# Score visits of one key chunk between second products, and two first-product tiles begun early at the seam of batch 0

## The chip, the cores and the metric

The kernel runs on one core of a Trainium2 chip. The metric is the device time of one execution in microseconds, the median of several runs. TensorE is called PE, its weight loads PEld, VectorE DVE, ScalarE ACT, GpSimd POOL. A program on one core has no second die to compare with. All runs used here were classed as fast; the few in which the granted clock was visibly below 1 are named where they matter.

## The reference

Attention with one added to the softmax denominator, followed by a two-layer network with a squared ReLU:

```python
scores = scale * np.matmul(q, k.transpose(0, 1, 3, 2))        # 8 batches, 12 heads, 448 x 64
m = np.max(scores, axis=-1, keepdims=True)
e = np.exp(scores - m)
attn = e / (np.sum(e, axis=-1, keepdims=True) + np.exp(-m) + 1e-09)
x = np.matmul(attn, v) ...                                    # as 3584 tokens x 768
h = x @ w_in                                                  # 768 x 2048, "first products"
r = np.maximum(h, 0.0)
return (r * r) @ w_out                                        # 2048 x 768, "second products"
```

## The kernel before

Heads are worked in pairs, six per batch, and the keys of a pair in four chunks of 112. A "visit" computes scores of some chunks into PSUM tiles named `sp` (two buffers); an exp on ACT empties each. First products are tiles of twelve matmul steps (six where a tile spans all 448 queries) into `mp` (three buffers), emptied by a ReLU (`rt`) and a square (`gs`) on DVE. Where one tile ends and the next begins is called a tile boundary below: there a product needs a free `mp` buffer.

Two parts matter. First, twelve stages, each of three pairs, in which visits alternate with second products. One step of a second product is two matmuls on the upper and lower 64 rows of the array ("row halves"); the scores use row halves too. Everything before and after a stage (values, first products, row sums) runs in "column halves", 64 columns of the array at a time.

```python
    for i in range(3 * NPAIR, NU, 3):
        b, pr = units[i][0:2]
        for j in range(3):
            begin(i + j)
            scores(units[i + j], ets[i + j], 0)          # chunks 0 and 1
            if j:
                add(i + j - 1, 1, 2)
            rows(10 if j < 2 else 9)                     # steps of second products
            scores(units[i + j], ets[i + j], 1)          # chunks 2 and 3
            add(i + j, 0)
            if j < 2:
                rows(10 if j < 1 else 9)
        mode[0] = COLS2
        for at in pending:
            take_in(at)                                  # values, normalised
        ...
```

Second, the seam: batch 0 is worked in two parts (queries 0 to 191, then 192 to 447), and when the first part is normalised its first products are queued and drained in portions between the attention groups that follow, up to the end of batch 1.

```python
        if i == NPAIR:                                   # the seam
            ...
            normalise(two, xp, rcp)
            scores(u, et, 1)
            keep_warm(2)                                 # two dummy matmuls
            queue(0, FIRST)
            share[0] = left() / (NPAIR + 4)
        else:
            for at in transpose_at.get(i, ()):
                transposes(*at)                          # each holds one mp buffer until DVE copies it
            if i == NPAIR + 1:
                scores(u, et, 1)
                values_of(i - 1, xp)
            drain(share[0] * 0.45)
            ...
```

At the end of batch 1 the queue must be empty before the first row-half stage begins (the second products need it):

```python
        for step in range(3):
            add_chunks(u, et, es, half, step)
            drain(share[0] * (0.15, 0.1, 0.15)[step])
        if i == 3 * NPAIR - 1:
            run(ins, len(ins))
            rcps[i] = row_sums([u], (ess.pop(i)[0:1],))
```

The softmax here doesn't subtract the row's maximum and nothing guards it: scores larger than these inputs give would overflow.

Of the kernel before, what the change touches and what calls it, by code (L numbers as in the profile page):

```python
# [9 lines left out]
FP16 = mybir.dt.float16  # L10
AF = mybir.ActivationFunctionType
ALU = mybir.AluOpType
# [3 lines left out]
def kernel(  # L16
# [9 lines left out]
    nc = tc.nc  # L26
# [114 lines left out]
            )  # L141


    def cast(b, pr, names="qk"):
        for name in names:
            f = flat.tile([P, 2, RUN, D], FP16, name=f"flat{name}")
            if pr < 2 and name == "k":
                nc.scalar.activation(out=f, in_=naturals[name, b, pr], func=AF.Copy)
            else:
                nc.vector.tensor_copy(f, naturals[name, b, pr])  # L150
            naturals[name, b, pr] = f

    def transposes(b, pr, between=None):
        tp = mp_tile(FP16)
        for i, name in enumerate("qk"):
            for s in range(RUN):
                for h in range(2):
                    nc.tensor.transpose(tp[64 * h:64 * h + 64, i, P * s:P * s + P],
                                        naturals[name, b, pr][:, h, s, :], ident[0:P, 0:P])
        if b not in qks:  # L160
            qks[b] = qk_pool.tile([128, 3, COLS], FP16, name="qk")
        if between:
            between()
        parts = (0, S // 2, S) if b == 0 and pr < 2 else (0, S)
        for x, y in zip(parts, parts[1:]):
            nc.vector.tensor_copy(qks[b][:, 0:2, pr * S + x:pr * S + y], tp[:, :, x:y])  # L166

# [9 lines left out]
            return et[:, 0:RUN * 2 * n].rearrange("p (c h j n) -> p c h j n", c=2, h=2, j=2)[:, c, :, kk % 2, :]  # L177
        return et.rearrange("p (k x) -> p k x", k=RUN)[:, kk]

    def scores(u, et, c):  # L180
        b, pr, q0, n = u
        qk = qks[b]
        two = [] if n == S else s_psum.tile([P, 2, 512], FP32, name="sp")
        for kk in (2 * c, 2 * c + 1):
            sp = s_psum.tile([P, 2, 512], FP32, name="sp") if n == S else two
            if b in ON_PE:
                o = 0 if n == S else kk % 2 * n
                for h in range(2):
                    r = slice(64 * h, 64 * h + 64)
                    x = pr * S  # L190
                    nc.tensor.matmul(sp[:, h, o:o + n], qk[r, 1, x + P * kk:x + P * kk + P],  # L191
                                     qk[r, 0, x + q0:x + q0 + n], start=True, stop=True)
            else:
                for h in range(2):
                    for odd in range(2):
                        r = slice(64 * odd, 64 * odd + 64)
                        x = (2 * pr + h) * (S // 2)
                        kx = x + kk // 2
                        which = 1
                        if kk % 2 != odd:  # L200
                            which = 2
                            kx += kk % 2
                        nc.tensor.matmul(sp[:, odd, h * (S // 2):(h + 1) * (S // 2)],  # L203
                                         qk[r, which, kx:kx + 2 * P - 1:2], qk[r, 0, x:x + S // 2],
                                         start=True, stop=True)
            if n == S:
                exp(chunk(et, u, c, kk).rearrange("p (o x) -> p o x", o=2), sp[:, :, 0:S])
        if n < S:
            exp(et[:, 0:RUN * 2 * n].rearrange("p (c h x) -> p c h x", c=2, h=2)[:, c], two[:, :, 0:2 * n])
# [74 lines left out]
    def product(out_, lhsT, rhs, start, stop):  # L284
# [4 lines left out]
        else:  # L289
            nc.tensor.matmul(out_, lhsT, rhs, start=start, stop=stop)  # L290

    def tile_in(t0, n, f0, per):

        xt, x0 = xts[t0 // S], t0 % S
        m = per * n
        hp = mp_tile()
        for j in range(per):
            fb = f0 + j
            for dc in range(DCH):
                product(hp[:, j * n:(j + 1) * n], win[:, dc, fb * 128:(fb + 1) * 128],  # L300
                        xt[:, dc, x0:x0 + n], start=(dc == 0), stop=(dc == DCH - 1))
                if j < per - 1 or dc < DCH - 1:
                    yield n / 2.4
        rt = r_pool.tile([128, 512], FP16, name="rt")
        nc.vector.tensor_scalar(out=rt[:, 0:m], in0=hp[:, 0:m], scalar1=0.0, scalar2=None, op0=ALU.max)  # L305
        r = rt[:, 0:m].rearrange("p (j n) -> p j n", j=per)
        nc.vector.tensor_mul(gs[:, f0:f0 + per, t0 % RING:t0 % RING + n], r, r)  # L307
        yield n / 2.4

    def store(c, ot, n0, n1):  # L310
        end = c + 128
# [68 lines left out]
    def queue(t0, n):  # L380

        per = max(1, 512 // n)
        for f0 in range(0, NFFB, per):
            ns = per * DCH * n / 2.4
            ins.append([ns, ns, tile_in(t0, n, f0, per)])

# [20 lines left out]
    def drain(ns):  # L407
        while ins and ns > 0:
            ns -= one(ins)
# [16 lines left out]
    def keep_warm(n):  # L426
        wp = m_psum.tile([128, 512], FP32, name="mp")
        for _ in range(n):
            nc.tensor.matmul(wp, warm[:, 0:128], warm, start=True, stop=True)
# [27 lines left out]
    def sums_of(at):  # L457
        return row_sums(units[at:at + 2], (ess.pop(at)[0:1], ess.pop(at + 1)[0:1]))

    def values_of(at, xp):  # L460
        values(units[at], ets.pop(at), xp, at % 2 * units[at][3])
# [9 lines left out]
    for i in range(NPAIR):  # L471
        u, et, es, half = begin(i)
        mode[0] = COLS2
        scores(u, et, 0)
        if i < 2:
            scores(u, et, 1)
        if i in (3, 5):
            rcp = sums_of(i - 3)
        if i == 0:
            transposes(0, 1, lambda: cast(0, 2, "q"))  # L480
            cast(0, 2, "k")
        else:
            for at in transpose_at.get(i, ()):
                transposes(*at)
        if i == 0:
            keep_warm(1)
        if i:
            sums(i - 1)
        if i > 1:
            scores(u, et, 1)  # L490
        if i in (2, 4):
            xp = x_psum.tile([128, 512], FP32, name="xp")
        if i in (2, 3, 4):
            values_of(i - 2, xp)
        if i == 4:
            values_of(3, xp)
        if i in (3, 5):
            normalise(units[i - 3:i - 1], xp, rcp)
        if i in (1, 3, 5):
            keep_warm(1 + i // 5)  # L500


    for i in range(NPAIR, 2 * NPAIR):
        u, et, es, half = begin(i)
        two = units[i - 2:i] if i % 2 == 0 else None
        if i % 2 or i == NPAIR:
            xp = x_psum.tile([128, 512], FP32, name="xp")
        mode[0] = COLS2
        scores(u, et, 0)
        if i == NPAIR:  # L510
            sums(i - 1)
            values_of(i - 2, xp)
            values_of(i - 1, xp)
            rcp = sums_of(i - 2)
            normalise(two, xp, rcp)
            scores(u, et, 1)
            keep_warm(2)
            queue(0, FIRST)
            share[0] = left() / (NPAIR + 4)
        else:  # L520
            for at in transpose_at.get(i, ()):
                transposes(*at)
            if i == NPAIR + 1:
                scores(u, et, 1)
                values_of(i - 1, xp)
            drain(share[0] * 0.45)
            if i > NPAIR + 1:
                scores(u, et, 1)
                values_of(i - 1, xp)
            if two:  # L530
                rcp = sums_of(i - 2)
            drain(share[0] * 0.3)
        add_chunks(u, et, es, half, 1)
        if two and i > NPAIR:
            normalise(two, xp, rcp)
        add_chunks(u, et, es, half, 2)
        if i > NPAIR:
            drain(share[0] * 0.25)
        if i == NPAIR + 5:
            load_natural(2, 0, 3)  # L540
            for n0 in (0, HALF):
                for j in range(2):
                    load_wout(n0, j, 2)
# [44 lines left out]
    def rows(n):  # L588
        mode[0] = ROWS2
        while outs and n > 0:  # L590
            one(outs)
            n -= 1
        mode[0] = COLS2
# [6 lines left out]
    def add(at, *steps):  # L600
        for step in steps:
            add_chunks(units[at], ets[at], *ess[at], step)
# [5 lines left out]
    for i in range(3 * NPAIR, NU, 3):  # L608
        b, pr = units[i][0:2]
        for j in range(3):  # L610
            begin(i + j)
            scores(units[i + j], ets[i + j], 0)
            if j:
                add(i + j - 1, 1, 2)
            rows(10 if j < 2 else 9)
            scores(units[i + j], ets[i + j], 1)
            add(i + j, 0)
            if j < 2:
                rows(10 if j < 1 else 9)
        mode[0] = COLS2  # L620
        for at in pending:
            take_in(at)
# [61 lines left out]
```

## Time and profile before

| | before |
|---|---|
| median time, first 3 runs (range) | 416.72 us (416.47 to 416.76) |
| span in the profile | 415.0 us |
| PE busy | 404.1 us, 97% |
| a row-half stage (the 2nd to 12th) | 10.45 us, eleven times (10.42 the first of them) |
| the first row-half stage | 68.89 to 80.12 us |

PE works almost throughout, so the question is what its turns contain. A matmul's record is longer than its turn: the reader takes the start of one group in the timeline and the start of the next, and compares like with like. The prediction below shows those lines. A line of a timeline gives the start, the length, the engine, the line of kernel.py, what is written and read, and how many instructions are merged in it (x4); square brackets give the idle time before it and what ended it.

### The profile page before, as it was taken

The page shows a single profiled execution, that of the slowest core. Times are in us where ns is not written, and L with a number is a line of the kernel's source. Part 1 is how long each engine was busy: PE and PEld are TensorE (multiplying, and loading weights), DVE is VectorE, ACT ScalarE, POOL GpSimd, SP SyncE. Part 2 cuts the span into 40 slices and gives each one's busy share as a digit, 9 for nine tenths or more (in the row PEclk, how much of TensorE's full clock was granted, in tenths as well). Part 3 has the DMA queues.
Part 4 walks back from the last instruction along what each step waited for, and adds up shares of the span by engine and source line. Part 5 has one row for each costly group of instructions (what it writes and reads, how often), then busy time and mean ns, then how long its engine had stood idle before and what let it go on. Part 6 is the DMA issues. An engine that isn't in the chain of part 4 may idle for free.

```text
span 415.0 us, 10686 instructions
## 1 busy us (share of the span) xinstructions
PE 404.1 (97%) x4717; PEld 271.7 (65%) x4717; DVE 289.8 (70%) x553; ACT 232.9 (56%) x312; POOL 36.7 (9%) x58
## 2 busy tenths in 40 slices
PE   7888999999999999999999999999999999999997
PEld 3566666867576766767676676767667675555664
DVE  4767988887866787776976788767876888287000
ACT  5888987758384655648464665837555573100111
POOL 7524030010000110002000040001000000000000
PEclk9999999999999999999999999999999999999999
DMA  9999999489204992398503984198101010000222
GB/s 201 197 197 198 203 202 218 87 155 207 71 16 93 171 190 51 87 191 145 134 2 88 190 145 97 55 187 142 42 2 39 39 40 2 38 39 0 77 76 77
DMA packets 75823, 45.58 MB, mean 110 GB/s; under 512 B 42560, under 2 KB 72000, under 8 KB 75456
## 3 DMA queue, kind: packets, MB, share of 16 engines
q0 software_dynamic: 28848, 22.16, 35.1%
q1 hardware_dynamic: 46208, 22.05, 23.5%
q8 instruction: 37, 0.61, 0.6%
q10 hardware_dynamic: 720, 0.69, 0.6%
q14 instruction: 10, 0.08, 0.1%
HBM read 45.69 MB, written 17.93 MB: 153 GB/s over the span
## 4 chain that ended last, share of the span: by engine, by line
PE 88%; ACT 4%; DVE 3%; DMA 3%; POOL 1%; issue 0%; POOLq 0%
PE mp L288 24%; PE mp L334 17%; PE mp L290 10%; PE xp L288 8%; PE sp L203 6%; PE mp L238 5%; PE xp L334 5%; PE xp L290 3%; PE xp L238 3%; ACT et L171 3%; DMA vn<-in_v_dram 3%; PE sp L191 2%; PE mp L252 2%; ACT rcp L255 1%; POOL nn L99 1%; DVE rt L305 1%
## 5 line engine op out<-in xcount | busy, mean ns | idle before, releaser
L171 ACT ACTIVATE et<-sp 112x896 f16<-112x896 f32 (+2 forms) x144 | 124.2, 913 | 49.8 <-PE sp L203 37.8
L288 PEld LDWEIGHTS <-win 128*64 128x64 f16 x1536 | 85.3, 110 | 45.0 <-issue 2.1
L288 PE MATMUL mp<-xt,win 128*64 128x448 f16 (+2 forms) x1200 | 107.1, 323 | 1.2 <-DVE qk L166 1.2
L334 PE MATMUL mp<-wout,gs 64*128 64x384 f16 x896 | 104.4, 322 | 0.2 <-DVE rt L305 0.2
L334 PEld LDWEIGHTS <-gs 64*128 64x128 f16 x1152 | 69.1, 94 | 19.6 <-issue 0.6
L305 DVE TENSOR_SCALAR rt<-mp 128x448 f16<-128x448 f32 (+2 forms) x96 | 59.7, 622 | 25.6 <-PE mp L288 13.1
L307 DVE TENSOR_TENSOR gs<-rt 128x448 f16<-128x448 f16 (+2 forms) x128 | 50.2, 392 | 4.4
L334 PE MATMUL xp<-wout,gs 64*128 64x384 f16 x256 | 48.0, 322 | 0.0
L255 ACT ACTIVATE rcp<-mp,one_b 128x448 f32<-128x448 f32 (+2 forms) x42 | 26.5, 630 | 37.7 <-PE mp L252 37.7
L171 ACT ACTIVATE nn<-sp 112x896 f16<-112x896 f32 x48 | 41.4, 914 | 6.0 <-PE sp L203 4.3
L343 ACT ACTIVATE ot<-mp 128x384 f32<-128x384 f32 (+1 forms) x16 | 7.6, 477 | 62.1 <-PE mp L290 48.2
L203 PE MATMUL sp<-qk 64*112 64x224 f16 x480 | 36.6, 260 | 0.0
L288 PE MATMUL xp<-xt,win 128*64 128x448 f16 x336 | 36.5, 352 | 0.0
L203 PEld LDWEIGHTS <-qk 64*112 64x112 f16 x480 | 29.6, 127 | 7.4 <-issue 3.6
L290 PEld LDWEIGHTS <-gs 128*128 128x128 f16 x256 | 24.4, 98 | 15.1 <-issue 0.4
L238 PEld LDWEIGHTS <-vn 112*64 112x64 f16 x432 | 22.4, 109 | 15.8 <-issue 3.8
L290 PE MATMUL mp<-wout,gs 128*128 128x384 f16 (+1 forms) x192 | 30.3, 317 | 0.0
L256 ACT ACTIVATE rcp<-rcp 128x448 f32<-128x448 f32 (+2 forms) x48 | 27.7, 577 | 1.5
L216 DVE TENSOR_TENSOR es<-et 112x896 f16<-112x896 f16 x30 | 18.7, 622 | 13.9 <-ACT et L171 13.8
L191 PE MATMUL sp<-qk 64*112 64x448 f16 (+2 forms) x192 | 24.6, 321 | 2.4 <-ACT et L171 1.4
L218 DVE TENSOR_TENSOR es<-es,half 112x896 f16<-112x896 f16 x42 | 26.2, 623 | 0.9
L341 DVE TENSOR_SCALAR ot<-mp 128x384 f32<-128x384 f32 x28 | 15.6, 558 | 14.4 <-PE mp L334 10.9
(63 smaller groups left out, 346.0 us busy)
## 6 DMA issues: line engine op xcount, KB each, us to landing
vn<-in_v_dram POOLq DMA_DIRECT2D x7, 672.0 KB, 8.7
out_dram<-ot SPq DMA_DIRECT2D x9, 384.0 KB, 2.3
win<-in_moe_w_in_dram POOLq DMA_DIRECT2D x8, 384.0 KB, 14.1
wout<-in_moe_w_out_dram POOLq DMA_DIRECT2D x4, 768.0 KB, 17.6
stage_q<-in_q_dram POOLq DMA_DIRECT2D x4, 676.0 KB, 10.7
stage_k<-in_k_dram POOLq DMA_DIRECT2D x4, 676.0 KB, 13.6
out_dram<-ot SPq DMA_DIRECT2D x8, 288.0 KB, 8.8
out_dram<-ot SPq DMA_DIRECT2D x9, 192.0 KB, 2.6
```

The lines of the kernel that those rows point to most:

```text
L171: nc.scalar.activation(out=out_, in_=in_, func=AF.Exp, scale=scale)
L191: nc.tensor.matmul(sp[:, h, o:o + n], qk[r, 1, x + P * kk:x + P * kk + P], qk[r, 0, x + q0:x + q0 + n], start=True, stop=True)
L203: nc.tensor.matmul(sp[:, odd, h * (S // 2):(h + 1) * (S // 2)], qk[r, which, kx:kx + 2 * P - 1:2], qk[r, 0, x:x + S // 2], start=True, sto ...
L218: nc.vector.tensor_add(es, es, half[:, 0:2 * S])
L238: nc.tensor.matmul(xp[64 * h:64 * h + 64, o:o + n], vns[b][:, 2 * pr + h, kk, :], of_head(chunk(et, u, kk // 2, kk), u, h), start=(kk == 0 ...
L255: nc.scalar.activation(out=rcp[:, 0:m], in_=zp[:, 0:m], func=AF.Ln, bias=one_b)
L256: nc.scalar.activation(out=rcp[:, 0:m], in_=rcp[:, 0:m], func=AF.Exp, scale=-1.0)
L288: nc.tensor.matmul(out_[x:x + 64], lhsT[:, x:x + 64], rhs, start=start, stop=stop)
L290: nc.tensor.matmul(out_, lhsT, rhs, start=start, stop=stop)
L305: nc.vector.tensor_scalar(out=rt[:, 0:m], in0=hp[:, 0:m], scalar1=0.0, scalar2=None, op0=ALU.max)
L307: nc.vector.tensor_mul(gs[:, f0:f0 + per, t0 % RING:t0 % RING + n], r, r)
L334: nc.tensor.matmul(o[:, 0:w], g[x:x + 64], wout[x:x + 64, fb, n0:n0 + w], start=(fb == 0), stop=(fb == NFFB - 1))
```

## The change

It has two aims: to let PE and ACT wait less for each other in the row-half stages, by giving each score chunk its own place between the second products; and to fill PE's wait at the seam with first products that need only the four pairs already normalised. The core of the diff (the moved ReLU helper and the unused `names` and `between` arguments are cut):

```diff
-            scores(units[i + j], ets[i + j], 0)
-            if j:
-                add(i + j - 1, 1, 2)
-            rows(10 if j < 2 else 9)
-            scores(units[i + j], ets[i + j], 1)
-            add(i + j, 0)
-            if j < 2:
-                rows(10 if j < 1 else 9)
+            for kk in range(RUN):
+                scores(units[i + j], ets[i + j], kk // 2, (kk % 2,))
+                if kk == 0 and j:
+                    add(i + j - 1, 1, 2)
+                if kk == 1:
+                    add(i + j, 0)
+                if (j, kk) != (2, RUN - 1):
+                    rows(5 if (RUN * j + kk) % 3 == 0 else 4)
...
+    def tiles_in_early(n, f0, per, ready):
+        xt = xts[0]
+        m = per * n
+        hps = [mp_tile(), mp_tile()]
+        for t, dcs in ((0, range(ready)), (1, range(ready)), (0, range(ready, DCH)), (1, range(ready, DCH))):
+            for j in range(per):
+                fb = f0 + per * t + j
+                for dc in dcs:
+                    product(hps[t][:, j * n:(j + 1) * n], win[:, dc, fb * 128:(fb + 1) * 128],
+                            xt[:, dc, 0:n], start=(dc == 0 and j == 0), stop=(dc == DCH - 1 and j == per - 1))
...
-            keep_warm(2)
...
-            if i == NPAIR + 1:
-                scores(u, et, 1)
-                values_of(i - 1, xp)
-            drain(share[0] * 0.45)
-            if i > NPAIR + 1:
-                scores(u, et, 1)
-                values_of(i - 1, xp)
+            drain(16 * FIRST / 2.4 if i == NPAIR + 1 else share[0] * 0.45)
+            scores(u, et, 1)
+            values_of(i - 1, xp)
...
-            transposes(0, 1, lambda: cast(0, 2, "q"))
-            cast(0, 2, "k")
+            cast(0, 2)                                   # after the transposes of pair 1
-        parts = (0, S // 2, S) if b == 0 and pr < 2 else (0, S)
+        parts = (0, S // 2, S) if b == 0 and pr < 3 else (0, S)
```

More of the change, by code (lines that the diff above doesn't have):

```diff
@@ L141, in transposed_loads, with cast @@
             )
-    def cast(b, pr, names="qk"):
-        for name in names:
+    def cast(b, pr):
+        for name in "qk":
             f = flat.tile([P, 2, RUN, D], FP16, name=f"flat{name}")
@@ L151, in cast, with transposes @@
             naturals[name, b, pr] = f
-    def transposes(b, pr, between=None):
+    def transposes(b, pr):
         tp = mp_tile(FP16)
@@ L161, in transposes @@
             qks[b] = qk_pool.tile([128, 3, COLS], FP16, name="qk")
-        if between:
-            between()
-        parts = (0, S // 2, S) if b == 0 and pr < 2 else (0, S)
+        parts = (0, S // 2, S) if b == 0 and pr < 3 else (0, S)
         for x, y in zip(parts, parts[1:]):
@@ L178, in chunk, with scores @@
         return et.rearrange("p (k x) -> p k x", k=RUN)[:, kk]
-    def scores(u, et, c):
+    def scores(u, et, c, only=(0, 1)):
         b, pr, q0, n = u
@@ L183, in scores @@
         two = [] if n == S else s_psum.tile([P, 2, 512], FP32, name="sp")
-        for kk in (2 * c, 2 * c + 1):
+        for kk in [2 * c + x for x in only]:
             sp = s_psum.tile([P, 2, 512], FP32, name="sp") if n == S else two
@@ L290, in product, with relu_squared @@
             nc.tensor.matmul(out_, lhsT, rhs, start=start, stop=stop)
+    def relu_squared(hp, t0, n, f0, per):
+        m = per * n
+        rt = r_pool.tile([128, 512], FP16, name="rt")
+        nc.vector.tensor_scalar(out=rt[:, 0:m], in0=hp[:, 0:m], scalar1=0.0, scalar2=None, op0=ALU.max)
+        r = rt[:, 0:m].rearrange("p (j n) -> p j n", j=per)
+        nc.vector.tensor_mul(gs[:, f0:f0 + per, t0 % RING:t0 % RING + n], r, r)
     def tile_in(t0, n, f0, per):
         xt, x0 = xts[t0 // S], t0 % S
-        m = per * n
         hp = mp_tile()
@@ L303, in tile_in @@
                     yield n / 2.4
-        rt = r_pool.tile([128, 512], FP16, name="rt")
-        nc.vector.tensor_scalar(out=rt[:, 0:m], in0=hp[:, 0:m], scalar1=0.0, scalar2=None, op0=ALU.max)
-        r = rt[:, 0:m].rearrange("p (j n) -> p j n", j=per)
-        nc.vector.tensor_mul(gs[:, f0:f0 + per, t0 % RING:t0 % RING + n], r, r)
+        relu_squared(hp, t0, n, f0, per)
         yield n / 2.4
+    def tiles_in_early(n, f0, per, ready):
+        xt = xts[0]
+        m = per * n
+        hps = [mp_tile(), mp_tile()]
[5 more added lines that the diff above has]
+                            xt[:, dc, 0:n], start=(dc == 0 and j == 0), stop=(dc == DCH - 1 and j == per - 1))
+                    if dc < DCH - 1 or j < per - 1:
+                        yield n / 2.4
+            if dcs[-1] == DCH - 1:
+                relu_squared(hps[t], 0, n, f0 + per * t, per)
+                yield n / 2.4
     def store(c, ot, n0, n1):
@@ L382, in queue @@
         per = max(1, 512 // n)
-        for f0 in range(0, NFFB, per):
+        first = 0
+        if t0 + n == FIRST:
+            first = 2 * per
+            ns = first * DCH * n / 2.4
+            ins.append([ns, ns, tiles_in_early(n, 0, per, DCH - 2)])
+        for f0 in range(first, NFFB, per):
             ns = per * DCH * n / 2.4
@@ L478 @@
             rcp = sums_of(i - 3)
+        for at in transpose_at.get(i, ()):
+            transposes(*at)
         if i == 0:
-            transposes(0, 1, lambda: cast(0, 2, "q"))
-            cast(0, 2, "k")
-        else:
-            for at in transpose_at.get(i, ()):
-                transposes(*at)
-        if i == 0:
+            cast(0, 2)
             keep_warm(1)
```

## The prediction

> **What bounds the kernel now.** I read the page first (shares, slices), then the busy time of each engine by window, then the timeline of TensorE and ScalarE in one repeating period, then the chain of waits and the timelines at the seam of batch 0.
>
> ```profile
> span 415.0 us, 10686 instructions
> PE 404.1 (97%) x4717; PEld 271.7 (65%) x4717; DVE 289.8 (70%) x553; ACT 232.9 (56%) x312; POOL 36.7 (9%) x58
> PEclk9999999999999999999999999999999999999999
> ...
> 209.00:221.00 12.00, 12.00 (x164) 9.02 (x162) 8.69 (x17) 9.70 (x12) 0.00 (x0) 1.00 0.14 36
> ```
>
> TensorE has work in flight 97% of the span at full clock; from 80 us on it has no recorded gap. In the window 209 to 221 us (columns: PE, weight loads, DVE, ACT, POOL) PE shows 12.00 of 12, with ACT the next at 9.70. But a matmul's record lasts longer than its turn, so short waits hide inside "busy". To see them I take the start of one group to the start of the next in a stage where score matmuls (L203) alternate with second products (L334) in row-half mode. There are twelve such stages, the first beginning at 68.89 us, the others like this one (209.56 to 220.01, that is 10.45 us):
>
> ```profile
> 213.63 0.57 PE L203 MATMUL sp<-qk 64*112 64x224 f16 x8
> 214.01 1.81 PE L334 MATMUL mp<-wout,gs 64*128 64x384 f16 x20
> 215.64 0.58 PE L203 MATMUL sp<-qk 64*112 64x224 f16 x8
> 216.02 0.52 PE L334 MATMUL mp<-wout,gs 64*128 64x384 f16 x4
> ...
> 217.48 0.74 PE L203 MATMUL sp<-qk 64*112 64x224 f16 x8
> 218.01 0.32 PE L334 MATMUL xp<-wout,gs 64*128 64x384 f16 x1
> ...
> 219.47 0.61 PE L203 MATMUL sp<-qk 64*112 64x224 f16 x8
> 220.01 0.95 PE L238 MATMUL mp<-et,vn 112*64 112x448 f16 x8
> ```
>
> A visit of two key chunks takes 0.38 us (213.63 to 214.01, 215.64 to 216.02), but 0.53 and 0.54 for the last two: about 0.15 us each is waiting. For what, ScalarE tells:
>
> ```profile
> 214.04 1.72 ACT L171 ACTIVATE et<-sp 112x896 f16<-112x896 f32 x2 [0.30 <-PE sp L203]
> 216.05 3.58 ACT L171 ACTIVATE et<-sp 112x896 f16<-112x896 f32 x4 [0.29 <-PE sp L203]
> ```
>
> Two exps take 1.72 us, one 0.91, so they start 0.81 apart. The first starts 0.41 us after its visit began (213.63, 214.04). There are two score buffers; a visit writes both, so its second chunk needs the previous visit's second exp finished, which is 0.41 + 1.72 = 2.13 us after that visit began, and reaches its turn at 1.63 + 0.38 + 0.19 = 2.20 when ten steps lie between, at about 2.04 when nine do. So ten are just enough and nine are not, which is where the waits stand. ACT also idles 0.3 us per visit: the pairing makes PE wait for ACT and ACT for PE in turn.
>
> At the seam the chain of waits runs over a DMA, ACT and DVE, not PE:
>
> ```profile
> 5.19 10.71 DMA vn<-in_v_dram
> ...
> 20.69 0.59 ACT rcp L255
> ...
> 21.74 1.01 ACT et L171
> ...
> 22.79 0.43 PE sp L191 x4
> ```
>
> ```profile
> 20.95 0.60 PE L429 MATMUL mp<-warm 128*128 128x512 f16 x2
> 21.48 0.43 PE L191 MATMUL sp<-qk 64*112 64x256 f16 x4
> 22.79 0.43 PE L191 MATMUL sp<-qk 64*112 64x256 f16 x4 [0.89 <-ACT et L171]
> 23.15 0.63 PE L238 MATMUL xp<-et,vn 112*64 112x256 f16 x8
> ...
> 35.75 0.27 PE L288 MATMUL mp<-xt,win 128*64 128x192 f16 x2 [1.08 <-DVE qk L166]
> ```
>
> PE does two dummy matmuls (L429), then waits 0.89 us for an exp, and the first useful first product comes at 23.61 us.
>
> **What the Trainium skill says.** "TensorE: Matmul & The Clock Gate", Back-to-back issue gap: N/2.4 + 2.5 ns for isolated warm matmuls; 384 columns give 162.5 ns, and twenty row-half matmuls, two at a time, take 1.63 us here: it agrees. "TensorEngine Tiling (Array Packing)", Tiling Modes: changing the mode drains TensorE. Scores and row-half products share the row split: ten steps and four-pair visits add up without a remainder, so the trace shows no cost of the extra switches. "PSUM — Partial Sum Buffer", The four PSUM rules: two accumulation groups open in one bank cannot both set the first flag; this is why the new early tiles set it on one product only; no run shows it yet. "Perfetto Trace Analysis", Identifying the Most-Contended Engine: matmul busy time is no measure of closeness to the roof; the 12.00 of 12 above hides the two waits, which agrees.
>
> **The change, part by part.**
>
> *1. Visits of one chunk.* No instruction is added. A stage keeps 12 chunks and 48 steps, with 5 or 4 steps after each chunk. A step is 0.1625 us, a chunk 0.19. Chunk to chunk is 0.19 + 4 x 0.1625 = 0.84 us at least, above ACT's 0.81, so exps don't queue. A chunk reuses the buffer of two before: at least 1.68 us later, while that exp ends 0.41 + 0.91 = 1.32 after its chunk began, plus about 0.05 of signalling (the 0.04 of issue that the chain shows between an exp and the scores): 0.3 us to spare. Both waits go: 0.53 + 0.54 - 2 x 0.38 = 0.31 us per stage, and after 80 us PE sets the end, so eleven stages give 11 x 0.305 = 3.4 us. The order on DVE shifts too: the last group's first addition stands before the last eviction instead of behind it. Its exps end 1.3 us after the chunk; the eviction is due about 1.65 us after, so it slips by some 0.3 us, and its buffer is wanted over a microsecond later: 0.
>
> *2. The first of these stages* (68.89 to 80.12, 11.2 us) has besides a wait for the exps in its second visit, about 0.44 us (the two exps come behind a reciprocal; the visit takes 0.82 instead of 0.38). Spread, PE gets three more steps done before it meets the same exps: about 0.4 back, plus its 0.31. It also waits for DVE before its first products, about 0.34, which I expect to stay in part. Counted: 0.5.
>
> *3. The seam.* The two dummies go (0.53 us), the second half of the next scores moves behind 16 first products (32 half matmuls of 192 columns, pairs of 82.5 ns: 1.3 us). They need only pairs 0 to 3, normalised by DVE at 19.24, and weights, no wait for which appears. The score group still stands at 22.8, because the exp before it ends at 22.75; but when values end at 23.61, 16 products are done instead of none. Six follow instead of eleven, so the next scores come at about 24.1 instead of 24.62: 0.5 us, and ACT, idle 0.52 us before its exp at 25.08, follows. From there the tile boundaries stand 11 products earlier. At 35.75 PE waited 1.08 us for a product buffer held by two transposes; now the boundary falls behind that group's scores and values, and I expect nearly all of that back, about 1.2 with its pipeline restart. So 1.7 us at 37 us. ACT then runs without a gap to 46.75 and carries it. At the end of batch 1 first products (from 66.25) 32 half matmuls stand instead of 46, 0.75 us less PE, but the row sums there need DVE, where one activation pair (1.1 us) now stands ahead of the last two additions; and in that group a boundary follows directly on two transposes, so a new wait of 0.2 to 0.9 us is likely. I let these cancel and count 1.6.
>
> *4. Casts and copies at the start* (order of one cast, one split copy): the chain hangs on the values' DMA that lands at 15.9 us; 0.
>
> Sum: 3.4 + 0.5 + 1.6 = 5.5 us; 416.7 - 5.5 = 411.2.
>
> **Rivals.**
> (a) ACT becomes the bound of the row stages: 12 exps at 0.81 are 9.7 us against PE's 12 x 0.19 + 48 x 0.1625 = 10.1. The four merged exps took 3.58, which includes a wait for PE, so 0.81 is their real pace. If waits cost ACT its pace and it ran at 0.90, 10.8 us would be longer than now and part 1 would give nothing: 414.5.
> (b) Each switch between scores and products costs something: eleven stages x 6 new visits x 0.03 would be 2 us, leaving 413.2. Against it: the sums above have no remainder.
> (c) The seam's gain is lost in DVE (9.44 of 10 us busy from 60 to 70 us) and in the new buffer wait: 412.8. I give this a quarter.
> (d) The seam gains all its waits, also that for a buffer at 58.95 (0.63 us): 410.
>
> **Range and chances.** The row stages are the safe part, 3.1 to 3.5; the seam with the first stage is 0.4 to 3.5. So 409.8 to 413.0 should hold it 8 times in 10. More than 2% faster is under 408.4, which would need 8.3 us, more than all the waits I found: 0.03. Slower by 2% would need a new wait in every stage: 0.01. Within 2%: 0.96.
>
> **What would show it.** Right: row stages of 10.15 us instead of 10.45, with every one-chunk visit at 0.19 (the first 0.05 more) and ACT without the 0.3 us gaps in pairs; first products starting at 21.3 us; the wait of 1.08 at 35.75 gone; the first row stage starting some 1.4 us earlier and ending 2 us earlier; from 80 us on the column stages unchanged. Wrong: waits of 0.1 us or more in one-chunk visits or a first product stretch of five steps above 0.82 (rival a or b); the first row stage starting where it did (c); anything new between a row stage and the values after it, from the DVE order.

## The result, and the profile after

The changed kernel takes 412.61 us in the median (412.40 to 413.03, 4 runs), the kernel before 416.74 us (416.47 to 417.32, 4 runs). The ratio is 0.9900, 95% interval 0.9883 to 0.9917. Ratios here are the mean time of one kernel's fast runs over that of the other's of the same rounds, so not quite the ratio of the medians quoted. The gain is 4.1 us, within 2%, and inside the range forecast; the point forecast was a gain of 5.5.

The head of the page of the changed kernel, and the window that holds one whole row-half stage (206.43 to 216.67 us), the same twelfth of the work as was shown of the kernel before:

```profile
span 410.6 us, 10685 instructions
PE 401.0 (98%) x4715; PEld 259.0 (63%) x4715; DVE 289.8 (71%) x554; ACT 234.4 (57%) x312; POOL 36.3 (9%) x58
...
206.00:218.00 12.00, 12.00 (x164) 8.14 (x162) 9.09 (x18) 10.48 (x12) 0.00 (x0) 1.00 0.14 36
```

PE is 12.00 of 12 in both, and yet the stage is shorter: the busy share says nothing of it. ACT's busy time in the window rose from 9.70 to 10.48, but mostly because the window of the kernel before cuts its last exp (0.63 us of it lie outside). Its timeline is clearer. Where the kernel before had pauses of 0.3 us, twelve exps now stand as one piece, without a pause long enough to be listed:

```profile
206.87 10.83 ACT L169 ACTIVATE et<-sp 112x896 f16<-112x896 f32 x12 [3.63 <-PE sp L201]
```

PE's timeline of that stage (L201 are the scores, L352 the second products, L236 the values that follow):

```profile
211.85 0.35 PE L201 MATMUL sp<-qk 64*112 64x224 f16 x4
212.04 0.97 PE L352 MATMUL mp<-wout,gs 64*128 64x384 f16 x10
212.86 0.35 PE L201 MATMUL sp<-qk 64*112 64x224 f16 x4
213.05 0.33 PE L352 MATMUL mp<-wout,gs 64*128 64x384 f16 x2
...
213.70 0.35 PE L201 MATMUL sp<-qk 64*112 64x224 f16 x4
...
216.38 0.35 PE L201 MATMUL sp<-qk 64*112 64x224 f16 x4
216.67 0.95 PE L236 MATMUL mp<-et,vn 112*64 112x448 f16 x8
```

A chunk takes 0.19 us (211.85 to 212.04, 212.86 to 213.05), five steps 0.82, four 0.65: as forecast. But the last one takes 0.29 (216.38 to 216.67), 0.09 or 0.1 too long, in each of the eleven stages. The stage is 10.24 us (10.21 the first of the eleven), not the 10.15 forecast.

At the seam and behind it:

```profile
20.85 1.51 PE L286 MATMUL mp<-xt,win 128*64 128x192 f16 x32
22.48 0.42 PE L189 MATMUL sp<-qk 64*112 64x256 f16 x4
...
33.67 0.58 PE L286 MATMUL mp<-xt,win 128*64 128x192 f16 x10
34.18 0.42 PE L189 MATMUL sp<-qk 64*112 64x256 f16 x4
...
35.87 0.59 PE L189 MATMUL sp<-qk 64*112 64x448 f16 x4
...
61.68 1.06 PE L286 MATMUL mp<-xt,win 128*64 128x256 f16 x16 [0.22 <-DVE qk L164]
...
67.21 0.38 PE L250 MATMUL mp<-es,ones 112*64 112x448 f16 x2 [1.13 <-DVE es L216]
67.52 0.40 PE L189 MATMUL sp<-qk 64*112 64x448 f16 x2
```

The first products begin at 20.85 instead of 23.61. The wait of 1.08 us at 35.75 is gone: behind ten half matmuls at 33.67 the scores follow at once. New are a small wait at 61.68, where a tile boundary now follows two transposes after one product (the kernel before waited 0.15 us in that group, at 64.37), and 1.13 us for the row sums' input at 67.21 (none before, at 68.60).

How far the changed kernel is ahead, at the same piece of work in both timelines:

| piece of work | before | after | ahead |
|---|---|---|---|
| scores of the group after the seam | 22.79 | 22.48 | 0.31 |
| first scores of batch 1 | 37.36 | 35.87 | 1.49 |
| scores of the last group of batch 1 | 61.85 | 59.86 | 1.99 |
| first row-half stage begins | 68.89 | 67.52 | 1.37 |
| first row-half stage ends | 80.12 | 78.10 | 2.02 |
| last row-half stage ends | 339.17 | 334.78 | 4.39 |
| end | 415.0 | 410.6 | 4.4 |

The 0.31 at the top is chance, as run 3 shows. Then come 1.7 us up to the end of the first stage, and 11 x 0.21 = 2.3 us from the other eleven. What lies between the stages, and the tail, is unchanged to within 0.1 us.

### The profile page after: what moved, and what is told of

It reads as the page before. It is cut to its first block, busy times and chain, and to the rows that moved or that the text cites. A ratio compares the mean times of both kernels' runs of the same rounds, so it can differ in the third digit from the quotient of the medians.

```text
span 410.6 us, 10685 instructions
## 1 busy us (share of the span) xinstructions
PE 401.0 (98%) x4715; PEld 259.0 (63%) x4715; DVE 289.8 (71%) x554; ACT 234.4 (57%) x312; POOL 36.3 (9%) x58
## 4 chain that ended last, share of the span: by engine, by line
PE 89%; ACT 4%; DVE 4%; DMA 1%; issue 1%
PE mp L286 24%; PE mp L352 17%; PE mp L288 11%; PE xp L286 8%; PE sp L201 6%; PE xp L352 5%; PE mp L236 5%; PE xp L288 3%; PE xp L236 3%; PE sp L189 3%; ACT et L169 3%; PE mp L250 2%; PE mp L158 1%; DMA et<-in_k_dram 1%; DVE qk L164 1%; ACT rcp L253 1%
## 5 line engine op out<-in xcount | busy, mean ns | idle before, releaser
L352 PE MATMUL mp<-wout,gs 64*128 64x384 f16 x896 | 115.2, 322 | 0.0
L286 PEld LDWEIGHTS <-win 128*64 128x64 f16 x1536 | 83.9, 110 | 45.6 <-issue 1.5
L352 PEld LDWEIGHTS <-gs 64*128 64x128 f16 x1152 | 58.1, 94 | 21.1
L352 PE MATMUL xp<-wout,gs 64*128 64x384 f16 x256 | 53.1, 323 | 0.0
L201 PE MATMUL sp<-qk 64*112 64x224 f16 x480 | 43.1, 258 | 0.0
L201 PEld LDWEIGHTS <-qk 64*112 64x112 f16 x480 | 30.6, 128 | 14.2 <-issue 3.6
L236 PEld LDWEIGHTS <-vn 112*64 112x64 f16 x432 | 22.4, 109 | 15.4 <-issue 3.9
L189 PE MATMUL sp<-qk 64*112 64x448 f16 (+2 forms) x192 | 25.8, 320 | 1.4 <-ACT et L169 0.6
L293 DVE TENSOR_SCALAR rt<-xp 128x448 f16<-128x448 f32 x32 | 19.9, 622 | 8.2 <-PE xp L286 6.7
## 6 DMA issues: line engine op xcount, KB each, us to landing
win<-in_moe_w_in_dram POOLq DMA_DIRECT2D x8, 384.0 KB, 14.2
```

Source lines behind the costliest of these rows:

```text
L189: nc.tensor.matmul(sp[:, h, o:o + n], qk[r, 1, x + P * kk:x + P * kk + P], qk[r, 0, x + q0:x + q0 + n], start=True, stop=True)
L201: nc.tensor.matmul(sp[:, odd, h * (S // 2):(h + 1) * (S // 2)], qk[r, which, kx:kx + 2 * P - 1:2], qk[r, 0, x:x + S // 2], start=True, sto ...
L236: nc.tensor.matmul(xp[64 * h:64 * h + 64, o:o + n], vns[b][:, 2 * pr + h, kk, :], of_head(chunk(et, u, kk // 2, kk), u, h), start=(kk == 0 ...
L286: nc.tensor.matmul(out_[x:x + 64], lhsT[:, x:x + 64], rhs, start=start, stop=stop)
L293: nc.vector.tensor_scalar(out=rt[:, 0:m], in0=hp[:, 0:m], scalar1=0.0, scalar2=None, op0=ALU.max)
L352: nc.tensor.matmul(o[:, 0:w], g[x:x + 64], wout[x:x + 64, fb, n0:n0 + w], start=(fb == 0), stop=(fb == NFFB - 1))
```

## The experiments

All twelve kernels passed the comparison with the reference, and each ran beside the kernel before on its own chip. Edits are against the kernel before ("before") or the changed one ("after").

### 1. The visits alone

Before, with only the first part of the diff above (`scores` with `only`, and the loop of four visits).

> Only the visits of one key chunk, nothing at the seam. Theory A (a stage loses 0.09 us to the switch from row halves to column halves whatever the order, so only about 0.21 us of waiting per stage can go): eleven stages of 10.24 us instead of 10.45, first stage about 0.7 shorter, 413.7 us. Rival B (the forecast: 0.31 us of waiting per stage goes, the last visit of the changed kernel is slowed by something at the seam): stages of 10.15, 412.8 us. Rival C (the gain of the stages needs the seam): above 415.

Measured: 413.96 us (413.72 to 414.18, 5 runs) against 416.62; ratio 0.9936 (0.9923 to 0.9948). The stages take 10.24 us and the first one 10.88. The visits alone give 2.7 us, and the slow last visit is theirs, not the seam's.

### 2. The seam alone

Before, with `tiles_in_early`, its queue, the new drain and without the two dummies.

> Only the seam: early first products, no two dummies, visits and casts as before. Theory A: the first stage begins 1.0 to 1.4 us earlier, and the stage keeps its own waits, so 415.4 us. Rival B (all of the 2.0 us by which the changed kernel is ahead after its first stage is the seam's): 414.7. Rival C (it is given back in the wait for the row sums just before the stage): 416.5.

Measured: 415.63 us (415.44 to 416.61, 5 runs) against 416.62; ratio 0.9984 (0.9970 to 0.9998). The seam alone gives 1.0 us, and its trace shows the same 1.13 us wait for the row sums. Adding up, 2.7 + 1.0 = 3.7 of 4.1; in the profiled runs 2.9 + 1.3 = 4.2 of 4.4. The rest is no larger than the spread of the runs.

### 3. The cast and the copy alone

Before, with only the last two pieces of the diff.

> Only the order of one cast and the split copy at the start. Theory A (the start hangs on the landing of the second values load, and its landing at 14.35 instead of 15.90 us in the changed kernel's trace is chance): 416.7 us, 0.1 either way. Rival B (the cast order lets that load land earlier, or the chain is elsewhere): 416.4 us, with the load at about 14.4 us again.

Measured: 416.68 us (416.65 to 416.94, 5 runs) against 416.62; ratio 1.0002 (0.9989 to 1.0014). The values' load landed at 15.87 us here, at 14.27 in the run with the visits alone, which has the old cast order: the landing is not decided by that order. How much of the start is chance, the traces of the kernels that share the changed start show (the changed one and runs 5 to 8, 10 and 11): the load lands between 14.2 and 16.0 us, and the scores just before the seam begin between 20.28 and 21.38 us (20.59 in the kernel before). The 0.31 us in the table is there already at those scores, and is well inside this scatter. So places in two traces are compared safely only when counted from those scores.

### 4. One number for the tile boundary

```diff
-            drain(share[0] * 0.45)
+            drain(4 * FIRST / 2.4 if i == NPAIR + 5 else share[0] * 0.45)
```

on the kernel before: four first products instead of five are drained between two transposes and the scores, in one group.

> The kernel before with one number changed: in the group where PE waits 1.08 us for a product buffer held by two transposes, four first products are drained ahead of the second scores instead of five, so that the tile boundary falls behind the scores. Theory A (much of the seam's gain is that boundary): the wait of 1.08 is gone, the scores behind it come about 1.2 us earlier, the time is 415.7 to 416.0. Rival B (another engine sets the pace there): the wait is gone and the time stays at 416.6 or more.

Measured: 415.07 us (415.03 to 415.55, 5 runs) against 416.62; ratio 0.9966 (0.9953 to 0.9978). One number gives 1.5 us, more than the 0.7 to 1.0 expected, and at least as much as the whole seam. Its timeline:

```profile
34.43 0.50 PE L288 MATMUL mp<-xt,win 128*64 128x192 f16 x8
34.86 0.43 PE L191 MATMUL sp<-qk 64*112 64x256 f16 x4
35.21 0.63 PE L238 MATMUL xp<-et,vn 112*64 112x256 f16 x8
36.01 0.69 PE L288 MATMUL mp<-xt,win 128*64 128x192 f16 x12 [0.17 <-DVE qk L166]
```

The product that opens a new tile, and so needs a buffer that a transpose still holds, now stands behind scores and values, and finds the buffer free after 0.17 us instead of 1.08. Later the wait of 0.63 us at 58.95 shrinks to 0.20 too.

### 5 and 6. A mode switch by itself

After, with one pair of tiny dummy matmuls before one chunk in the middle of each stage; their result is written over by the scores. In the first kernel they use column halves, in the second row halves.

```diff
+            if dummy:                                    # one chunk of each stage; column halves
+                for x in (0, 64):
+                    nc.tensor.matmul(sp[x:min(x + 64, P), 0, 0:64], warm[:, x:min(x + 64, P)], warm[:, 0:64], start=True, stop=True)
```

```diff
+            if dummy:                                    # the same in row halves
+                for x in (0, 64):
+                    nc.tensor.matmul(sp[:, x // 64, 0:64], warm[x:x + 64, 0:P], warm[x:x + 64, 0:64], start=True, stop=True)
```

> The changed kernel with one pair of tiny dummy matmuls (64 columns of data) in column halves put before one score chunk in the middle of each row-half stage, written over by the scores that follow. Theory A (going from row halves to column halves and back costs about 0.09 plus 0.14 us whatever is waited for): each of the twelve stages grows by about 0.25 us, so 415.5 us. Rival B (the longer last visit of a stage is a wait for a buffer or for DVE, and the switch is free): each grows by 0.03, 413.0 us.

> The control: the same dummy pair in row halves, so that the mode does not change. Both theories: each stage grows by 0.03 us, 413.0 us. If it grows by 0.2 or more, the dummy itself costs it and the other run tells nothing of the switch.

Measured: 416.10 us (415.91 to 416.25, 4 runs) with column halves, 413.26 (413.12 to 414.08, 4 runs) with row halves, both beside 416.82 of before; ratios 0.9980 and 0.9916. The stages take 10.53 and 10.29 us. The same two matmuls cost 0.05 us when the mode stays and 0.29 when it changes twice, so the two switches cost 0.24 us, and 12 x 0.24 = 2.9 agrees with the difference of the medians, 2.84. In the timeline with column halves (L186 the dummy, L204 scores):

```profile
189.43 0.81 PE L355 MATMUL mp<-wout,gs 64*128 64x384 f16 x8
190.17 0.22 PE L186 MATMUL sp<-warm 128*64 128x64 f16 x2
190.32 0.40 PE L204 MATMUL sp<-qk 64*112 64x224 f16 x4
190.56 0.49 PE L355 MATMUL mp<-wout,gs 64*128 64x384 f16 x4
```

Four steps before the dummy take 0.74 us instead of 0.65: 0.09 for the way from row halves to column halves. The rest, some 0.15, is paid on the way back, in the dummy's own turn and in the first chunk behind it (0.24 us instead of 0.19).

The same amounts stand at the borders of every stage, where there are no dummies. In the changed kernel the last pair of first products before each of the eleven stages takes 0.29 us instead of 0.19, and the first chunk 0.24 instead of 0.19; at the end it is the 0.09 or 0.1 of the last chunk. So the dummies' own shape is not the cause. The weight loads (PEld) show one thing more at the end of a stage:

```profile
216.22 0.29 PEld L201 LDWEIGHTS <-qk 64*112 64x112 f16 x4
216.67 0.33 PEld L236 LDWEIGHTS <-vn 112*64 112x64 f16 x6 [0.15 <-issue]
```

The weights of the last chunk are loaded from 216.22 on, 0.16 us before its matmuls (216.38); those of the values start together with their matmuls (216.67). Whether the 0.09 us is the emptying of the array or this load, which does not run ahead over the change, these runs do not separate.

### 7. A stage that ends with products

```diff
-                if (j, kk) != (2, RUN - 1):
-                    rows(5 if (RUN * j + kk) % 3 == 0 else 4)
+                rows(4)
```

on the changed kernel: four steps after every chunk, the last too.

> The changed kernel with four second-product steps after every chunk, the last included, so that a stage ends with products and not with scores. Theory A (mode switch): the last visit takes 0.19 us instead of 0.283, and the 0.09 us reappears between the last step and the values; the stage stays 10.24, the time 412.6. Rival B (the values wait for the last chunk's exp, its buffer or the eviction): the 0.09 us is gone or larger than 0.3; 411.6 or above 413.5.

Measured: 412.77 us (412.69 to 413.26, 4 runs) against 416.82; ratio 0.9904 (0.9888 to 0.9921). The end of a stage:

```profile
216.08 0.35 PE L201 MATMUL sp<-qk 64*112 64x224 f16 x4
216.27 0.32 PE L352 MATMUL xp<-wout,gs 64*128 64x384 f16 x1
...
216.76 0.32 PE L352 MATMUL xp<-wout,gs 64*128 64x384 f16 x1
216.76 0.32 PE L352 MATMUL mp<-wout,gs 64*128 64x384 f16 x1
217.01 0.76 PE L236 MATMUL mp<-et,vn 112*64 112x448 f16 x6
```

The last chunk takes its 0.19 us (216.08 to 216.27), and the last step takes 0.25 (216.76 to 217.01) instead of 0.16. The 0.09 us belongs to whatever stands last before the values. The last chunk's buffer and exp are not its cause, since that chunk now stands four steps earlier.

### 8. Fewer products in the groups, more at the end (did not help)

```diff
-            share[0] = left() / (NPAIR - 0.2)
+            share[0] = left() / (NPAIR + 1)
```

on the changed kernel.

> A version meant to beat both: the changed kernel, with 18 instead of 20 first products drained in each group of batch 1, and the rest left for the run at the end, where PE waits 1.13 us for the row sums; the boundary that stood right behind two transposes moves too. If the theory of the seam holds (PE sets the pace in those groups, and the two new waits cost 1.3 us): both waits gone, the first row stage 1 to 1.6 us earlier, 411.2 us. Rival (ACT and DVE set the pace of the groups): no group gets shorter, 412.6 or more.

Measured: 413.01 us (412.84 to 413.32, 4 runs) against 416.82; ratio 0.9907 (0.9892 to 0.9922). No gain: my reading that PE alone sets the pace of these groups was wrong. The wait for the row sums did fall, to 0.4 us, but with less product work between them the exps come as a closed block, and PE meets DVE's copies:

```profile
48.47 0.38 PE L250 MATMUL mp<-es,ones 112*64 112x448 f16 x2 [0.32 <-DVE qk L164]
...
58.68 0.38 PE L250 MATMUL mp<-es,ones 112*64 112x448 f16 x2 [0.52 <-DVE qk L164]
```

```profile
55.99 3.52 ACT L169 ACTIVATE et<-sp 112x896 f16<-112x896 f32 x4 [0.16 <-PE sp L189]
```

### 9. The visits and the one number, without the seam

Before, with the edits of 1 and 4.

> The kernel before with only the visits of one chunk and the one changed number of the boundary run; no early products, the dummies kept, casts as before. Theory A (the early start of the two tiles is worth no more than the boundary that it happens to move): gains add up, 416.7 - 2.7 - 1.5, so 412.4 to 412.6 us, the same as the changed kernel. Rival B (the early products give something of their own): 413.2 or more.

Measured: 412.28 us (412.09 to 412.71, 4 runs) against 416.62; ratio 0.9896 (0.9880 to 0.9913). Without any early product this is at least as fast as the changed kernel.

### 10. The last group of batch 1 reordered: a version that beats both

```diff
+        last = i == 3 * NPAIR - 1
         for step in range(3):
             add_chunks(u, et, es, half, step)
-            drain(share[0] * (0.15, 0.1, 0.15)[step])
-        if i == 3 * NPAIR - 1:
-            run(ins, len(ins))
+            if not last:
+                drain(share[0] * (0.15, 0.1, 0.15)[step])
+        if last:
+            drain(left() - 250.0)
             rcps[i] = row_sums([u], (ess.pop(i)[0:1],))
+            run(ins, len(ins))
```

on the changed kernel.

> The changed kernel with the last group of batch 1 reordered: its three additions stand before the activation pair of the next-to-last tile, and its row sums before the last two products. Theory A (the wait of 1.13 us for the row sums and the late exps behind it are only this order on DVE): the wait is gone, the first row stage begins about 1 us earlier and its wait of 0.33 for an exp goes, 411.6 us. Rival B (DVE's work in that group sets the pace in any order): 412.4 or more.

Measured: 411.60 us (411.37 to 411.77, 4 runs) against 416.62; ratio 0.9878 (0.9863 to 0.9893). In the changed kernel DVE has a ReLU of the next-to-last tile ahead of the additions, and that ReLU waits for PE:

```profile
63.13 0.62 DVE L214 TENSOR_TENSOR es<-et 112x896 f16<-112x896 f16 x1
64.81 0.69 DVE L293 TENSOR_SCALAR rt<-mp 128x512 f16<-128x512 f32 x1 [1.06 <-PE mp L286]
65.53 0.42 DVE L295 TENSOR_TENSOR gs<-rt 128x512 f16<-128x512 f16 x1
65.88 0.62 DVE L214 TENSOR_TENSOR half<-et 112x896 f16<-112x896 f16 x1
```

In the reordered one the addition starts as soon as its exps end, and the row sums wait 0.35 us instead of 1.13:

```profile
64.90 0.63 DVE L214 TENSOR_TENSOR half<-et 112x896 f16<-112x896 f16 x1 [1.12 <-ACT et L169]
```

```profile
66.24 0.38 PE L250 MATMUL mp<-es,ones 112*64 112x448 f16 x2 [0.35 <-DVE es L216]
66.45 0.39 PE L286 MATMUL mp<-xt,win 128*64 128x256 f16 x4
66.77 0.40 PE L189 MATMUL sp<-qk 64*112 64x448 f16 x2
```

The first stage begins at 66.77 instead of 67.52, both traces having the same start (20.31 and 20.28 at the scores before the seam). The stage itself is hardly shorter (10.55 against 10.58): its wait of 0.33 us for an exp is gone, as expected, but 0.20 us before its first products and 0.09 in its last visit have come in its place.

### 11. The boundary put back

```diff
-            drain(16 * FIRST / 2.4 if i == NPAIR + 1 else share[0] * 0.45)
+            drain(16 * FIRST / 2.4 if i == NPAIR + 1 else 6 * FIRST / 2.4 if i == NPAIR + 5 else share[0] * 0.45)
```

on the changed kernel.

> The changed kernel with the boundary put back: in the group with two transposes six first products are drained instead of five ahead of the second scores, so that one product again asks for a new buffer right behind the two transposes. Theory A (the seam's gain is mostly the boundary that the early tiles moved): a wait of about 1 us for a transpose's buffer is back and the time is 413.5 to 414.0 us, that of the visits alone. Rival B (the early products give the gain): 412.5 to 412.9.

Measured: 414.24 us (414.00 to 414.77, 6 runs) against 416.70; ratio 0.9925, with a wide interval (0.9889 to 0.9961), since two runs of the kernel before beside it took 418.07 and 421.45, at granted clocks of 0.996 and 0.983; the medians are not touched by them. The wait is back:

```profile
34.52 0.58 PE L286 MATMUL mp<-xt,win 128*64 128x192 f16 x10
36.10 0.27 PE L286 MATMUL mp<-xt,win 128*64 128x192 f16 x2 [1.00 <-DVE qk L164]
```

The time is that of the visits alone, even with the early products. In this trace the wait for the row sums before the first stage has grown from 1.1 to 1.7 us, and the wait of 0.6 us for a copy that the kernel before had is back too.

### 12. The reordering without the early products

Before, with the edits of 1, 4 and 10.

> The kernel before with the visits, the one changed number of the boundary, and the same reordering of the last group of batch 1 as in the best version so far (411.6), but without the early products. Theory A (the early products give something once the wait for the row sums behind them is gone): 412.0 to 412.3 us, behind the best version by 0.4 to 0.7. Rival B (they give nothing in any order, and the reordering alone made the best version): 411.6 us or less.

Measured: 412.14 us in the median of 6 runs. Two of them (416.41 and 416.46, the profiled one among them) had a mean granted clock of 0.984 and 0.983; the other four took 411.94 to 412.19, so the printed ratio of 0.9904 is not used, nor the trace. The four are about 0.5 us behind those of kernel 10; but that ran on another chip, and against the kernel before beside it each gains about the same: 4.8 us here, 5.0 there. By time alone the early products give something between 0.2 and 0.5 us in this order, which the spread hardly lets one see.

The traces at full clock say more, if places are counted from the scores just before the seam:

| us after those scores | last group of batch 1 | first row-half stage begins | and ends |
|---|---|---|---|
| before | 41.26 | 48.30 | 59.53 |
| 2, the seam alone | 39.57 | 47.23 | 58.45 |
| 4, one number | 39.93 | 46.74 | 57.96 |
| 9, visits and one number | 39.93 | 46.73 | 57.49 |
| the changed kernel | 39.58 | 47.24 | 57.82 |
| 10, reordered | 39.58 | 46.46 | 57.00 |

With early products (2, changed, 10) the last group of batch 1 begins 0.35 us earlier than with the one number alone (4, 9), the same in every trace. In the order of the changed kernel this is more than lost before the first stage, which then begins 0.5 us later than without early products; in the order of run 10 it begins 0.27 us earlier.

## Why the prediction was right or wrong

**The bound, and the visits: right in mechanism, a third too large.** PE sets the end of the eleven stages, the chunk-to-chunk rhythm of 0.84 us is above ACT's pace of 0.81, no one-chunk visit in the middle waits, and no switch between scores and second products costs anything. The term that failed is "0.53 + 0.54 - 2 x 0.38 = 0.31 us per stage"; it measured 0.21. Of the two long visits, the 0.54 of the last was taken for waiting throughout. About 0.09 of it is the array going from row halves to column halves for the values, which the new order pays as well (runs 5 to 7). So only about 0.06 of the last visit's excess was waiting, and 0.15 of the other's. The prediction cited "TensorEngine Tiling (Array Packing)", Tiling Modes, that a mode change drains the array, looked only at the switches that the change adds (there are none of that kind), and did not ask which of the waits it counted stood at a mode change. Eleven stages at 0.21 instead of 0.31 are 1.1 of the 1.4 us by which the point was missed.

**The first stage: right in size, partly by luck.** 0.5 us was expected; it went from 11.23 to 10.58, 0.65 us. But the visits alone give only 0.35 (run 1). There the wait of 0.44 us for exps went, as forecast, while the wait for DVE before the first second products did not stay "in part": it grew from 0.34 to 0.53 us. In the changed kernel it is the other way round, no wait for DVE and 0.33 us for an exp, after PE has waited 1.13 us for the row sums just before the stage. So part of the 0.65 was paid for ahead of the stage.

**The seam: too large, and not in its shares.** 1.6 us was expected; the table gives 1.37 up to the first stage, 0.31 of it chance, so about 1.1. The wait of 1.08 did vanish by the moved boundary, as forecast, and that boundary is the gain (runs 4, 9, 11): a single number without the early tiles does at least the same. Of the 0.5 us given to the early products 0.35 is there up to the last group of batch 1 (the table under run 12), and then the order of work in that group, on DVE above all, takes more than that back; run 10, which changes this order alone, wins 0.8 us. The prediction named both new waits (a boundary behind two transposes, the ReLU ahead of the additions) and let them cancel against the missing products of the last run, 0.75 us; they came out at 0.22 and 1.13 us, 0.6 more than that.

**The start: right.** Run 3 gives 0. The chain hung on the values' load in the kernel before, where PE waits 0.3 us for it; in the changed kernel's trace the load landed at 14.35 us and is not waited for.

**The early tiles' flag: right.** The prediction took it from "PSUM — Partial Sum Buffer", The four PSUM rules, that of several groups open in one bank only one may set the first flag (the page says: in one bank and the same quadrant of partitions, as here). The changed kernel does so and its result is correct. No run sets the flag on all of them.

**The rivals.** (a) and (b) are out: in the eleven stages every visit between the first and the last takes 0.19 us, and the five or four steps ahead of it 0.82 or 0.65, so none waits for ACT and no switch costs time. (c), the seam's gain lost in DVE, is partly what happened. (d) is out by the time, though the wait of 0.63 at 58.95 is gone; one of 0.20 us stands a group earlier instead.

## What to carry to other kernels

Before counting a long turn as a wait, ask what stands next to it: a turn at the border of two array modes contains the switch, and no reordering inside the mode removes it. When a queue is drained in portions between other work, look at where its buffer boundaries fall; one that falls right behind transposes cost more here than a reordering of whole tiles won, and one number moved it. And follow a gain to the next place where the engines meet: what the early products won at the seam was lost 45 us later to the order of a few instructions, most of them on another engine. Last, when two traces are compared, count from a piece of work behind the start: here the start alone scattered by over 1 us among kernels that share it.

## What the Trainium skill lacked or had wrong

- "TensorEngine Tiling (Array Packing)", Tiling Modes, says that changing the mode drains the array, but gives no cost. Here a change from row halves to column halves costs 0.09 us and the pair of changes 0.24 us (stages of 10.53 against 10.29 us), 2.84 us in twelve stages. Nor does it say that weights are not loaded ahead over such a change: here they are loaded 0.16 us ahead within a mode, and together with their matmul behind the change (216.67).
- The same page lists 64×128 among its modes, but does not say outright whether a smaller matmul in it, such as 64x112, counts as the same mode. Here scores on 64x112 and products on 64x128 alternate without any cost: 0.19 us a chunk and 0.65 us for four steps, with twelve as with six visits a stage.
